# Banded attention with sinks, then a gated feed-forward: sink weights of all heads in one product per pair of heads

## The chip, the cores and the metric

The kernel runs on one core of a Trainium2 chip. The metric is the time of one execution on the device in microseconds (us), from the median of several executions. The engines are TensorE (PE in the profile; PEld is its weight load), VectorE (DVE), ScalarE (ACT), GpSimd (POOL) and SyncE (SP), which here issues the DMA transfers. Matmul results land in PSUM; everything else lives in SBUF.

## The reference

```python
batch, n_heads, seq, head_dim = (4, 8, 768, 64);  n_sink, window = (4, 128)
scores = scale * np.matmul(q, k.transpose(0, 1, 3, 2))
is_sink = pos[None, :] < int(n_sink)
in_window = (rel >= 0) & (rel < int(window))        # rel = query position - key position
a = softmax of scores where (is_sink | in_window), else masked
attn_out = np.matmul(a, v)
x = attn_out.transpose(0, 2, 1, 3).reshape(B * S, H * D)      # (3072, 512)
gate = 1.0 / (1.0 + np.exp(-(x @ w_gate)));  val = x @ w_val   # d_ff = 1536
out = gate * val @ w_out                                       # (3072, 512)
```

All inputs are float32 (the feed-forward weights arrive as float64 and are decoded in the kernel). `n_sink` and `window` are inputs; a slow general path takes over if they lie outside what the fast path is built for.

## The kernel before, in words

**Two parts that run into each other.** Attention is done in units called attends: one head of one batch and two tiles of 128 queries. There are 4 batches x 3 groups of two tiles x 8 heads = 96 attends, numbered `u`. Eight consecutive attends (one group) give the 512 rows of `x`, transposed, for two tiles. The feed-forward then runs over chunks of tiles (`MT`: four tiles, two, then six chunks of three), for each of twelve slices `f` of `d_ff`: up-projections into `m` (`feed_part`, L1057), tanh gating (`th`, `gh`, `gl`), down-projections into `o`.

**Precision.** A float32 product is made of float32r parts: a value is split in a high part and the rest, and a product is high x high + low x high + high x low. `copy` (L505) makes the high part on ACT or DVE, `rest` (L516) the low part on POOL or DVE (DVE alone if the source is in PSUM). The first 16 attends (`PLAIN`) use plain float32 matmuls instead, which are recorded as two instructions each.

**One attend** (`attend`, L697). Loads of q, k and v; k carries the first `NS` = 16 keys after each tile of 128, so a tile has `KW` = 144 key columns. Scores go to a PSUM tile `a`; one DVE instruction merges the two tiles of the window (`tri`), one applies mask and maximum; ACT takes the exponential with the row sum `rs`; after the guard and the reciprocal all 144 columns of `P` are multiplied by it. `turn` (L799) transposes on PE, per query tile, the 128 window columns and the 16 sink columns: four transposes. The window part goes through ACT, DVE and POOL to `wt`. The sink part, 16 rows x 256 queries, is copied to `sk`, and its rest is made on DVE (not in plain attends). `pv` (L876) multiplies by the values: two or three matmuls for the window and one more of 256 columns for the sinks, with the stationary `vshl`, in the same accumulation. ACT and DVE add the high and low halves into `xr`, 64 rows for each head of a pair.

**From attention to the feed-forward.** After each second head (`if h % 2`, L932) `xr` is split into `XH[:, c]` and `XL[:, c]`, `c` = pair of heads. `XH` and `XL` are a ring of `RING` = 6 tiles. The up-projection of a chunk is cut in halves: the first reads pairs 0 and 1, the second pairs 2 and 3. In plain attends `xr` is a PSUM tile `a`; there are three buffers of tag `a` (`B_a`), used by scores, transposes and pv results. Outside plain attends `xr` is in SBUF, three buffers of 256 columns.

**The sinks' values** (`sinks`, L663): per batch, four small loads of v into `VSRAW`, a copy and a rest into one of two `VSHL`.

**The order.** `Plan.run` (L285) is a list scheduler on the host. It holds estimated durations for all operations and writes out one order per engine, by priority: an attend has priority `u`, its operations' engines may be alternatives; decoding of weight slices has due times in units of `u` (the last about 25); on PE the feed-forward has priority 10000 and more, so it fills what attention leaves. Up to 130 us (`WARM`), PE gets filler matmuls (`m<-ident`) where it would be idle. Because engines run in the written order, an instruction that waits holds up those behind it on its engine. All planned instructions go through one helper line, L484, so groups in the profile are told apart by their tiles.

Of the kernel before, what the change touches and what calls it, by code (L numbers as in the profile page):

```python
# [19 lines left out]

NS = 16
WIN = 128
# [3 lines left out]
RING = 6  # L26
# [4 lines left out]
PLAIN = 16  # L31
SINKP = -2.0
SCALP = -0.5
# [25 lines left out]
B_small = 1  # L59
B_xr = 3  # L60
B_th = 2
B_g = 2
# [6 lines left out]
BUFS = {}  # L69
# [361 lines left out]
def kernel(  # L431
# [3 lines left out]
    k: bass.AP,  # L435
    v: bass.AP,
    n_sink: bass.AP,
    window: bass.AP,
# [118 lines left out]
    nc.gpsimd.memset(VSRAW(), 0.0)  # L557
    for x in SK:
        nc.vector.tensor_copy(out=x(), in_=VSRAW().rearrange("p h d -> p (h d)"))

# [30 lines left out]
    def places():  # L591
        G.iota(
            mk()[:, 0:128], [[-1, 128]], base=0, channel_multiplier=1,
            allow_small_or_imprecise_dtypes=True,
        )
        G.iota(
            mk()[:, 128:144], [[1, NS]], base=0, channel_multiplier=0,
            allow_small_or_imprecise_dtypes=True,
        )
# [15 lines left out]
    def first_mask():  # L615

        rel, col, ge = mk()[:, 0:128], mk()[:, 128:144], mk()[:, 144:272]
        inw, snk, s0 = mk()[:, 272:400], mk()[:, 400:416], mk()[:, 416:432]
        V.scalar_tensor_tensor(
            out=inw, in0=rel, scalar=win, in1=ge, op0=ALU.is_lt, op1=ALU.mult  # L620
        )
        V.tensor_scalar(out=snk, in0=col, scalar1=nsk, scalar2=None, op0=ALU.is_lt)
        V.tensor_tensor(out=s0, in0=snk, in1=inw[:, 0:NS], op=ALU.is_gt)
        low(am[0][:, 0:128], inw)
        low(am[0][:, 128:KW], s0)

    def later_masks():


        rel, relm, inm = mk()[:, 0:128], mk()[:, 432:560], mk()[:, 560:688]  # L630
        snk, inp = mk()[:, 400:416], mk()[:, 688:704]
        V.tensor_scalar(out=inm, in0=relm, scalar1=win, scalar2=None, op0=ALU.is_lt)
# [27 lines left out]
    chunk_of = [i for i, parts in enumerate(MT) for _ in range(sum(parts))]  # L660
    VS = {}

    def sinks(b, u):  # L663
        raw, vs = VSRAW, VSHL[b % 2]
        VS[b] = raw, vs
# [6 lines left out]
        u = max(u, PLAIN)  # L672
        copy(u + SINKP, H // 2 * D, lambda: vs()[:, :, 0:D], raw, [raw], [(vs, 0)])
# [22 lines left out]

    def attend(u, b, h, t0, T, XR):  # L697

# [16 lines left out]
        else:  # L715
# [11 lines left out]
            qk_reads, qk_ns = [qs, kh, kl], 2  # L727

        P = tile([128, T, KW], F32, "P", BUFS["P"])
        rs = tile([128, 4], F32, "rs", BUFS["P"])  # L730
# [44 lines left out]
        for t in range(T):  # L775
            plan.op(
                u, [
                    ("V", 390, lambda t=t: V.tensor_scalar(
                        out=P()[:, t], in0=P()[:, t], scalar1=rs()[:, t : t + 1], scalar2=None,
                        op0=ALU.mult,  # L780
                    )),
                    ("A", 320, lambda t=t: A.mul(out=P()[:, t], in_=P()[:, t], mul=rs()[:, t : t + 1])),
                    ("G", 450, lambda t=t: G.tensor_scalar(
                        out=P()[:, t], in0=P()[:, t], scalar1=rs()[:, t : t + 1], scalar2=None,
                        op0=ALU.mult,
                    )),
                ][::-1],
                [rs], [(P, t)],
            )


# [30 lines left out]

        plan.op(u, [("PE", 30 + 2 * T * 110, turn)], [P], [tp, wt], busy=0.45)
        plan.op(
# [11 lines left out]

        o = 64 * (h % 2)
        if plain:
            vhl = vraw
            sk = tile([128, W], F32, "low", BUFS["small"])  # L840
            copy(u, W, lambda: sk()[o : o + NS], lambda: tp()[0:NS, W : 2 * W], [tp], [sk], True)
        else:
            sk = SK[h % 2]
# [15 lines left out]
        acc = None if plain else tile([128, 512], F32, "a", BUFS["a"], ps)  # L859
        if h % 2 == 0:  # L860
            XR[0] = tile([128, 512], F32, "a", BUFS["a"], ps) if plain else tile([128, W], F32, "xr", BUFS["xr"])
        xr = XR[0]
# [10 lines left out]

        vs = VS[b][0] if plain else VS[b][1]

        def pv():  # L876
            a = (xr()[e : e + D] if plain else acc())[:, 0 : Z * W].rearrange("p (z x) -> p z x", z=Z)
            for i, (_, l, c0, r0, n) in enumerate(blocks):
                PE.matmul(
                    a[:, :, c0 : c0 + n], lhsT=vhl()[:, l],  # L880
                    rhs=w().rearrange("p z t x y -> p z (t x y)")[:, :, r0 : r0 + n],
                    start=i == 0, stop=False, skip_group_check=True,
                )
            if plain:
                sv, sw = vs()[o : o + NS, h // 2], sk()[o : o + NS]
            else:
                sv, sw = vs()[:, h // 2], sk()[:, 0:W]
            PE.matmul(
                a[:, 0], lhsT=sv, rhs=sw, start=False, stop=True, skip_group_check=True
            )  # L890

        e = (h % 2) * D
        if plain:
            plan.op(
                u, [("PE", sum(5 + 4 * n / 2.4 for n in [W] + [x[-1] for x in blocks]), pv)], [vs, sk, vhl, wt],
                [(xr, h % 2)],
            )
        else:
            low = tile([D, W], F32, "low", BUFS["small"])
            plan.op(  # L900
                u, [("PE", mac(W) + sum(mac(2 * n) for *_, n in blocks), pv)],
                [vs, sk, vhl, wt], [acc, low, (xr, h % 2)],
            )
# [15 lines left out]
            else:  # L919
# [7 lines left out]
                u, [("V", vec(W), lambda: V.tensor_tensor(  # L927
                    out=xr()[e : e + D], in0=acc()[0:D, W : 2 * W], in1=low(), op=ALU.add
                ))],
                [acc, low], [(xr, h % 2)],  # L930
            )
        if h % 2:  # L932

            c, g = h // 2, b * NT + t0
            runs = [[0]]
            for t in range(1, T):
                if chunk_of[g + t] == chunk_of[g + t - 1]:
                    runs[-1].append(t)
                else:
                    runs.append([t])  # L940
            for run in runs:
                cols = slice(run[0] * 128, run[-1] * 128 + 128)
                ts = slice((g + run[0]) % RING * 128, (g + run[0]) % RING * 128 + len(run) * 128)
                parts = [(c, (g + t) % RING) for t in run]
                x = lambda cols=cols: xr()[:, cols]
                hi, lo = lambda ts=ts: XH()[:, c, ts], lambda ts=ts: XL()[:, c, ts]
                copy(u, len(run) * 128, hi, x, [xr], [(XH, p) for p in parts], plain)
# [5 lines left out]
    def f0(prev):  # L953
        return 1 - prev

# [178 lines left out]
    for b in range(B):  # L1134
        t0 = 0
        for T in AT[b]:
            XR = [None]
            for h in range(H):
                attend(u, b, h, t0, T, XR)
                u += 1  # L1140
# [34 lines left out]

_INS = ["q", "k", "v", "n_sink", "window", "moe_w_gate", "moe_w_val", "moe_w_out"]
_OUTS = [((3072, 512), "float32")]
# [37 lines left out]
```

## Time and profile before

| | |
|---|---|
| median of 3 runs | 828.9 us (827.07 to 831.28) |
| profiled execution, span from first to last instruction | 828.5 us |
| PE busy | 808.2 us, 98% |
| DVE busy | 527.2 us, 64% |
| POOL busy | 450.6 us, 54% |
| ACT busy | 417.9 us, 50% |
| moved by DMA | 95.31 MB, mean 115 GB/s |

The profile of an execution gives its span and no other time; the median lies 0.4 us above it. Matmuls are pipelined, so a matmul's length in a row overlaps the next one's; the distance between starts tells what it costs. Groups are written as line, engine, operation, written tile <- read tiles, shapes, count, busy us, mean ns, and the idle time before them with what ended it.

### The profile page before, as it was taken

The page shows a single profiled execution, that of the slowest core. Times are in us where ns is not written, and L with a number is a line of the kernel's source. Part 1 is how long each engine was busy: PE and PEld are TensorE (multiplying, and loading weights), DVE is VectorE, ACT ScalarE, POOL GpSimd, SP SyncE. Part 2 cuts the span into 40 slices and gives each one's busy share as a digit, 9 for nine tenths or more (in the row PEclk, how much of TensorE's full clock was granted, in tenths as well). Part 3 has the DMA queues.
Part 4 walks back from the last instruction along what each step waited for, and adds up shares of the span by engine and source line. Part 5 has one row for each costly group of instructions (what it writes and reads, how often), then busy time and mean ns, then how long its engine had stood idle before and what let it go on. Part 6 is the DMA issues. An engine that isn't in the chain of part 4 may idle for free.

```text
span 828.5 us, 15445 instructions
## 1 busy us (share of the span) xinstructions
PE 808.2 (98%) x4804; PEld 729.3 (88%) x4804; DVE 527.2 (64%) x1610; ACT 417.9 (50%) x1197; POOL 450.6 (54%) x610
## 2 busy tenths in 40 slices
PE   8999999999999999999999999999999999999996
PEld 6667688888999989999899999999989999999995
DVE  5767689898899898936941499856951485111111
ACT  3666788986668766624630376634730272001001
POOL 4656578899676777725651387755741383111110
PEclk8999999999999999999999999999999999999998
DMA  5667767784645444323431253433431141112112
GB/s 142 173 178 201 214 170 219 218 231 143 180 126 131 125 122 119 108 81 94 127 96 38 54 153 92 121 96 93 127 95 41 36 115 32 44 35 88 40 38 67
DMA packets 99256, 95.31 MB, mean 115 GB/s; under 512 B 44384, under 2 KB 79200, under 8 KB 99168
## 3 DMA queue, kind: packets, MB, share of 16 engines
q1 hardware_dynamic: 99168, 94.25, 41.1%
q8 instruction: 41, 0.67, 0.3%
q14 instruction: 47, 0.39, 0.2%
HBM read 84.77 MB, written 9.44 MB: 114 GB/s over the span
## 4 chain that ended last, share of the span: by engine, by line
PE 67%; DVE 9%; ACT 3%; DMA 2%; POOL 2%; issue 2%; SPq 1%; DVEq 0%; ACTq 0%; POOLq 0%
PE m L484 38%; PE o L484 18%; PE a L484 10%; DVE sk L484 1%; DVE w L484 1%; DMA vraw<-in_v_dram 1%; SPq L484 1%; ACT P L484 1%; DVE vhl L484 1%; DVE wt L484 1%; DVE P L484 1%; DVE xr L484 1%; DVE a L484 1%; DMA qkT<-in_k_dram 1%; POOL P L484 1%
## 5 line engine op out<-in xcount | busy, mean ns | idle before, releaser
L484 POOL TENSOR_TENSOR gl<-th,gh 128x384 fp32r<-128x384 f32 (+1 forms) x73 | 70.8, 971 | 206.8 <-DVE gh L484 196.9
L484 DVE SCALAR_TENSOR_TENSOR th<-th,m 128x384 f32<-128x384 f32 (+1 forms) x108 | 54.6, 505 | 198.9 <-PE m L484 198.2
L484 ACT ACTIVATE th<-m 128x384 f32<-128x384 f32 (+1 forms) x108 | 49.3, 457 | 232.9 <-PE m L484 218.8
L484 POOL TENSOR_SCALAR_AFFINE_SELECT wt<-wt 128x512 fp32r<-128x512 f32 (+3 forms) x192 | 117.0, 610 | 51.6 <-DVE wt L484 31.5
L484 PE MATMUL m<-XH,wvh 128*128 128x384 f32 (+1 forms) x432 | 140.1, 324 | 0.6 <-ACT th L484 0.6
L484 PE MATMUL m<-XH,wgh 128*128 128x384 f32 (+1 forms) x432 | 140.2, 325 | 0.0
L484 PE MATMUL m<-XL,wvh 128*128 128x384 f32 (+1 forms) x432 | 137.4, 318 | 0.0
L484 PE MATMUL m<-XL,wgh 128*128 128x384 f32 (+1 forms) x432 | 137.4, 318 | 0.0
L484 PE MATMUL m<-XH,wgl 128*128 128x384 f32 (+1 forms) x432 | 137.3, 318 | 0.0
L484 PE MATMUL m<-XH,wvl 128*128 128x384 f32 (+1 forms) x432 | 137.3, 318 | 0.0
L484 PE MATMUL o<-woh,gh 128*128 128x512 f32 x276 | 110.6, 401 | 0.0
L484 PE MATMUL o<-woh,gl 128*128 128x512 f32 x276 | 108.5, 393 | 1.0 <-DVE gl L484 0.5
L484 PE MATMUL o<-wol,gh 128*128 128x512 f32 x276 | 107.8, 391 | 0.5 <-DMA wol<-wol_d 0.5
L484 ACT ACTIVATE P<-P,negm_all 128x144 f32<-128x144 f32 x192 | 78.8, 411 | 26.2 <-DVE negm_all L484 23.7
L484 PEld LDWEIGHTS m<-XH,wvh 128*128 128x128 f32 x432 | 81.5, 189 | 3.7 <-ACT th L484 0.8
L484 PEld LDWEIGHTS m<-XH,wgh 128*128 128x128 f32 x432 | 81.4, 188 | 3.0 <-issue 0.7
L484 PEld LDWEIGHTS m<-XL,wvh 128*128 128x128 f32 x432 | 81.6, 189 | 1.4
L484 PEld LDWEIGHTS m<-XL,wgh 128*128 128x128 f32 x432 | 81.5, 189 | 1.2
L484 PEld LDWEIGHTS m<-XH,wvl 128*128 128x128 f32 x432 | 81.4, 189 | 0.0
L484 PEld LDWEIGHTS m<-XH,wgl 128*128 128x128 f32 x432 | 81.4, 188 | 0.0
L484 DVE CUSTOM_DVE_ANT_0 P<-a,am 128x144 f32<-128x144 f32 x192 | 58.6, 306 | 9.6 <-PE a L484 3.2
L484 PEld LDWEIGHTS o<-woh,gl 128*128 128x128 f32 x276 | 51.7, 187 | 14.0 <-POOL gl L484 1.3
(116 smaller groups left out, 1727.1 us busy)
## 6 DMA issues: line engine op xcount, KB each, us to landing
wol<-wol_d SPq DMA_DIRECT2D x108, 256.0 KB, 2.9
qkT<-in_k_dram SPq DMA_DIRECT2D x120, 108.0 KB, 2.7
qkT<-in_q_dram SPq DMA_DIRECT2D x176, 64.0 KB, 2.5
wst<-in_moe_w_gate_dram SPq DMA_DIRECT2D x12, 512.0 KB, 4.6
wst<-in_moe_w_val_dram SPq DMA_DIRECT2D x12, 512.0 KB, 4.5
wst<-in_moe_w_out_dram SPq DMA_DIRECT2D x12, 512.0 KB, 4.0
vraw<-in_v_dram SPq DMA_DIRECT2D x64, 96.0 KB, 2.3
out_dram<-w SPq DMA_DIRECT2D x23, 256.0 KB, 2.5
```

The costliest lines, as they stand in the source:

```text
L484: return lambda *a, **kw: tc.keep_in_program_order(op(*a, **kw))
```

## The change

`NS` becomes 4, so `KW` is 132: k loads, scores, masks and exponentials are 12 columns narrower per tile. The normalising multiplication covers only the 128 window columns. The four sink columns of each head are multiplied by `rs` in an instruction of their own, into `psk`, which gathers all eight heads of a group. `turn` and `pv` no longer deal with sinks. After the eighth head a new function `join` transposes `psk` (32 columns per query tile, two transposes), puts the high part twice and the rest once into the 96 rows of `sk`, and multiplies it, in one matmul per pair of heads, by `VSP`: 32 rows of high values, the same again, 32 rows of the low values. The host passes the sinks' values as an extra input, laid out so that each row has values only in the columns of its own head. A sum on DVE adds the product to `xs` (four heads, 512 columns, three buffers), and only then are `XH` and `XL` made, two pairs at a time. In plain attends the pv result is copied to `xs` by ACT. `VSP` has one buffer for all batches; its load goes through a buffer of tag `w2`.

```diff
-NS = 16
+NS = 4
-SINKP = -2.0
+SINK0 = 1.5
+B_psk = 2
+B_sk = 2
...
-    VSRAW = Fixed(const.tile([128, H // 2, D], F32, name="vsraw"))
-    VSHL = [Fixed(const.tile([128, H // 2, 2 * D], F32R, name=f"vshl{i}")) for i in range(2)]
-    SK = [Fixed(const.tile([128, 256], F32R, name=f"sk{i}")) for i in range(2)]
...
+    NR = H * NS
+    VSP = Fixed(const.tile([3 * NR, H // 2, 2 * D], F32R, name="vsp"))
...
     def sinks(b, u):
-        raw, vs = VSRAW, VSHL[b % 2]
-        for o in range(0, 128, 32):
-            dma(
-                u if u < PLAIN else u + SINKP, 91.0, lambda o=o: Q.dma_start(
-                    out=raw()[o : o + NS], in_=v[b, o // 64 :: 2, 0:NS, :].rearrange("h p d -> p h d"),
-                ), w=[(raw, o)],
-            )
...
+        raw = tile([3 * NR, H // 2, 2 * D], F32, "w2", BUFS["w2"])
+        vs = VSP
+        pr = u + SINK0
+        dma(pr, 600.0, lambda: Q.dma_start(out=raw(), in_=v_sink[b]), w=[raw, vs])
+        copy(pr, H * D, vs, raw, [raw], [vs])
         rest(
-            u + SINKP, H // 2 * D, lambda: vs()[:, :, D : 2 * D], raw, lambda: vs()[:, :, 0:D],
-            [raw, (vs, 0)], [(vs, 1)],
+            pr, H * D, lambda: vs()[2 * NR : 3 * NR], lambda: raw()[2 * NR : 3 * NR],
+            lambda: vs()[2 * NR : 3 * NR], [raw], [vs],
         )
...
-                        out=P()[:, t], in0=P()[:, t], scalar1=rs()[:, t : t + 1], scalar2=None,
+                        out=P()[:, t, 0:128], in0=P()[:, t, 0:128], scalar1=rs()[:, t : t + 1],
...
+        def sink_weights(E):
+            return lambda: E.tensor_tensor(
+                out=psk()[:, 0:T, h], in0=P()[:, 0:T, 128:KW],
+                in1=rs()[:, 0:T].unsqueeze(2).to_broadcast([128, T, NS]), op=ALU.mult,
+            )
+        plan.op(
+            u, [("V", 110, sink_weights(V)), ("G", 400, sink_weights(G))], [rs, (P, T)], [(psk, h)]
+        )
...
-                PE.transpose(
-                    out=tp()[0:NS, W + t * 128 : W + t * 128 + 128], in_=P()[:, t, 128:KW],
-                    identity=ident,
-                )
...
-            copy(
-                u, W, lambda: sk()[o : o + NS, 0:W], lambda: tp()[0:NS, W : 2 * W], [tp], [(sk, 0)],
-                True,
-            )
-            rest(
-                u, W, lambda: sk()[o + 32 : o + 32 + NS, 0:W], lambda: tp()[0:NS, W : 2 * W],
-                lambda: sk()[o : o + NS, 0:W], [tp, (sk, 0)], [(sk, 1)], True,
-            )
...
-            PE.matmul(
-                a[:, 0], lhsT=sv, rhs=sw, start=False, stop=True, skip_group_check=True
-            )
...
+            if h % 2:
+                plan.op(
+                    u, [("A", act(W, True), lambda: A.copy(out=xs()[:, c], in_=xr()[:, 0:W]))], [xr],
+                    [(xs, (c, 0)), (xs, (c, 1))],
+                )
...
-        if h % 2:
+        if h == H - 1:
+            join(u, b, t0, T, XS, psk)
+
+    def join(u, b, t0, T, XS, psk):
+        W, g, vs = T * 128, b * NT + t0, VSP
+        ts = tile([128, 512], F32, "a", BUFS["a"], ps)
+        sk = tile([3 * NR, W], F32R, "sk", BUFS["sk"])
+        def turn():
+            for t in range(T):
+                PE.transpose(
+                    out=ts()[0:NR, t * 128 : t * 128 + 128],
+                    in_=psk()[:, t].rearrange("p h s -> p (h s)"), identity=ident,
+                )
+        plan.op(u, [("PE", 30 + T * 110, turn)], [psk], [ts, sk], busy=0.45)
+        for i in (0, 2):
+            plan.op(
+                u, [("A", act(W, True), lambda i=i: A.copy(
+                    out=sk()[i * NR : i * NR + NR], in_=ts()[0:NR, 0:W]
+                ))],
+                [ts], [(sk, i)],
+            )
+        rest(
+            u, W, lambda: sk()[NR : 2 * NR], lambda: ts()[0:NR, 0:W], lambda: sk()[0:NR],
+            [ts, (sk, 0)], [(sk, 1)], True,
+        )
...
+        for i, xs in enumerate(XS):
+            sp = tile([128, 512], F32, "a", BUFS["a"], ps)
...
+            def add(i=i, spv=spv):
+                for c in range(2):
+                    PE.matmul(
+                        spv()[:, c], lhsT=vs()[:, 2 * i + c], rhs=sk(), start=True, stop=True,
+                    )
+            plan.op(u, [("PE", 2 * mac(W), add)], [vs, sk], [sp])
+            plan.op(
+                u, [("V", vec(2 * W), lambda spv=spv, xs=xs: V.tensor_tensor(
+                    out=xs(), in0=spv(), in1=xs(), op=ALU.add
+                ))],
+                [sp], [xs],
+            )
...
+                copy(u, n, hi, x, [xs], [(XH, p) for p in parts])
                 rest(
-                    u, len(run) * 128, lo, x, hi, [xr] + [(XH, p) for p in parts],
-                    [(XL, p) for p in parts], plain,
+                    u, n, lo, x, hi, [xs] + [(XH, p) for p in parts], [(XL, p) for p in parts]
                 )
...
+        if name == "v_sink":
+            t = _np.zeros((a.shape[0], 3, a.shape[1], NS, a.shape[1] // 2, 2, a.shape[3]), a.dtype)
+            for h in range(a.shape[1]):
+                t[:, :, h, :, h // 2, h % 2] = a[:, None, h, :NS]
```

More of the change, by code (lines that the diff above doesn't have):

```diff
@@ L436 @@
     v: bass.AP,
+    v_sink: bass.AP,
     n_sink: bass.AP,
@@ L551 @@
     XL = Fixed(const.tile([128, NC, RING * 128], F32R, name="XL"))
-    VSRAW = Fixed(const.tile([128, H // 2, D], F32, name="vsraw"))
-    VSHL = [Fixed(const.tile([128, H // 2, 2 * D], F32R, name=f"vshl{i}")) for i in range(2)]
-    SK = [Fixed(const.tile([128, 256], F32R, name=f"sk{i}")) for i in range(2)]
-    nc.gpsimd.memset(VSRAW(), 0.0)
-    for x in SK:
-        nc.vector.tensor_copy(out=x(), in_=VSRAW().rearrange("p h d -> p (h d)"))
+    NR = H * NS
+    assert NR == 32
+    VSP = Fixed(const.tile([3 * NR, H // 2, 2 * D], F32R, name="vsp"))
     val = keep.tile([128, 2], F32, name="val")
@@ L596, in places @@
         G.iota(
-            mk()[:, 128:144], [[1, NS]], base=0, channel_multiplier=0,
+            mk()[:, 128 : 128 + NS], [[1, NS]], base=0, channel_multiplier=0,
             allow_small_or_imprecise_dtypes=True,
@@ L615, in first_mask @@
     def first_mask():
-        rel, col, ge = mk()[:, 0:128], mk()[:, 128:144], mk()[:, 144:272]
-        inw, snk, s0 = mk()[:, 272:400], mk()[:, 400:416], mk()[:, 416:432]
+        rel, col, ge = mk()[:, 0:128], mk()[:, 128 : 128 + NS], mk()[:, 144:272]
+        inw, snk, s0 = mk()[:, 272:400], mk()[:, 400 : 400 + NS], mk()[:, 416 : 416 + NS]
         V.scalar_tensor_tensor(
@@ L630, in later_masks @@
         rel, relm, inm = mk()[:, 0:128], mk()[:, 432:560], mk()[:, 560:688]
-        snk, inp = mk()[:, 400:416], mk()[:, 688:704]
+        snk, inp = mk()[:, 400 : 400 + NS], mk()[:, 688 : 688 + NS]
         V.tensor_scalar(out=inm, in0=relm, scalar1=win, scalar2=None, op0=ALU.is_lt)
@@ L695, in load, with attend @@
         )
-    def attend(u, b, h, t0, T, XR):
+    def attend(u, b, h, t0, T, XR, XS, PSK):
         prev = 1 if t0 else 0
@@ L727, in attend @@
             qk_reads, qk_ns = [qs, kh, kl], 2
+        if h == 0:
+            PSK[0] = tile([128, T, H, NS], F32, "psk", BUFS["psk"])
+        psk = PSK[0]
         P = tile([128, T, KW], F32, "P", BUFS["P"])
@@ L778, in attend @@
                     ("V", 390, lambda t=t: V.tensor_scalar(
-                        out=P()[:, t], in0=P()[:, t], scalar1=rs()[:, t : t + 1], scalar2=None,
-                        op0=ALU.mult,
-                    )),
-                    ("A", 320, lambda t=t: A.mul(out=P()[:, t], in_=P()[:, t], mul=rs()[:, t : t + 1])),
+                        out=P()[:, t, 0:128], in0=P()[:, t, 0:128], scalar1=rs()[:, t : t + 1],
+                        scalar2=None, op0=ALU.mult,
+                    )),
+                    ("A", 320, lambda t=t: A.mul(
+                        out=P()[:, t, 0:128], in_=P()[:, t, 0:128], mul=rs()[:, t : t + 1]
+                    )),
                     ("G", 450, lambda t=t: G.tensor_scalar(
-                        out=P()[:, t], in0=P()[:, t], scalar1=rs()[:, t : t + 1], scalar2=None,
-                        op0=ALU.mult,
+                        out=P()[:, t, 0:128], in0=P()[:, t, 0:128], scalar1=rs()[:, t : t + 1],
+                        scalar2=None, op0=ALU.mult,
                     )),
@@ L821, in split @@
             )
-        plan.op(u, [("PE", 30 + 2 * T * 110, turn)], [P], [tp, wt], busy=0.45)
+        plan.op(u, [("PE", 30 + T * 110, turn)], [P], [tp, wt], busy=0.45)
         plan.op(
@@ L835, in attend @@
         plan.op(u, [("G", 1100.0 if plain else 1400.0, split)], [], [wt])
-        o = 64 * (h % 2)
         if plain:
             vhl = vraw
-            sk = tile([128, W], F32, "low", BUFS["small"])
-            copy(u, W, lambda: sk()[o : o + NS], lambda: tp()[0:NS, W : 2 * W], [tp], [sk], True)
-        else:
-            sk = SK[h % 2]
-            copy(
-                u, W, lambda: sk()[o : o + NS, 0:W], lambda: tp()[0:NS, W : 2 * W], [tp], [(sk, 0)],
-                True,
-            )
-            rest(
-                u, W, lambda: sk()[o + 32 : o + 32 + NS, 0:W], lambda: tp()[0:NS, W : 2 * W],
-                lambda: sk()[o : o + NS, 0:W], [tp, (sk, 0)], [(sk, 1)], True,
-            )
+        else:
             vhl = tile([128, L, 2 * D], F32R, "vhl", BUFS["vhl"])
@@ L859, in attend @@
         acc = None if plain else tile([128, 512], F32, "a", BUFS["a"], ps)
-        if h % 2 == 0:
-            XR[0] = tile([128, 512], F32, "a", BUFS["a"], ps) if plain else tile([128, W], F32, "xr", BUFS["xr"])
+        if h % 4 == 0:
+            XS.append(tile([128, 2, W], F32, "xr", BUFS["xr"]))
+        xs, c = XS[-1], h // 2 % 2
+        if plain and h % 2 == 0:
+            XR[0] = tile([128, 512], F32, "a", BUFS["a"], ps)
         xr = XR[0]
@@ L872, in attend @@
         assert blocks[0][-1] == W
-        vs = VS[b][0] if plain else VS[b][1]
         def pv():
@@ L881, in pv @@
                     rhs=w().rearrange("p z t x y -> p z (t x y)")[:, :, r0 : r0 + n],
-                    start=i == 0, stop=False, skip_group_check=True,
+                    start=i == 0, stop=i == len(blocks) - 1, skip_group_check=True,
                 )
[L884 to L887, printed above, removed]
-            PE.matmul(
-                a[:, 0], lhsT=sv, rhs=sw, start=False, stop=True, skip_group_check=True
-            )
         e = (h % 2) * D
@@ L894, in attend @@
             plan.op(
-                u, [("PE", sum(5 + 4 * n / 2.4 for n in [W] + [x[-1] for x in blocks]), pv)], [vs, sk, vhl, wt],
-                [(xr, h % 2)],
-            )
+                u, [("PE", sum(5 + 4 * n / 2.4 for *_, n in blocks), pv)], [vhl, wt], [(xr, h % 2)]
+            )
+            if h % 2:
[3 more added lines that the diff above has]
+                )
         else:
@@ L900, in attend @@
             plan.op(
-                u, [("PE", mac(W) + sum(mac(2 * n) for *_, n in blocks), pv)],
-                [vs, sk, vhl, wt], [acc, low, (xr, h % 2)],
+                u, [("PE", sum(mac(2 * n) for *_, n in blocks), pv)],
+                [vhl, wt], [acc, low, (xs, (c, h % 2))],
             )
@@ L927, in attend @@
                 u, [("V", vec(W), lambda: V.tensor_tensor(
-                    out=xr()[e : e + D], in0=acc()[0:D, W : 2 * W], in1=low(), op=ALU.add
+                    out=xs()[e : e + D, c], in0=acc()[0:D, W : 2 * W], in1=low(), op=ALU.add
                 ))],
-                [acc, low], [(xr, h % 2)],
+                [acc, low], [(xs, (c, h % 2))],
             )
-        if h % 2:
[L934 to L940, printed above, removed]
+        if h == H - 1:
+            join(u, b, t0, T, XS, psk)
@@ new lines, in join @@
+    def join(u, b, t0, T, XS, psk):
[20 more added lines that the diff above has]
+        )
+        runs = [[0]]
+        for t in range(1, T):
+            if chunk_of[g + t] == chunk_of[g + t - 1]:
+                runs[-1].append(t)
+            else:
+                runs.append([t])
+        for i, xs in enumerate(XS):
+            sp = tile([128, 512], F32, "a", BUFS["a"], ps)
+            spv = lambda sp=sp: sp()[:, 0 : 2 * W].rearrange("p (c x) -> p c x", c=2)
+            def add(i=i, spv=spv):
[10 more added lines that the diff above has]
+            )
@@ L941, in attend @@
             for run in runs:
                 cols = slice(run[0] * 128, run[-1] * 128 + 128)
[L943 to L947, printed above, removed]
+                k = (g + run[0]) % RING * 128
@@ L948, in attend @@
+                ts_ = slice(k, k + len(run) * 128)
+                parts = [(c, (g + t) % RING) for t in run for c in (2 * i, 2 * i + 1)]
+                x = lambda cols=cols, xs=xs: xs()[:, :, cols]
+                hi = lambda ts_=ts_, i=i: XH()[:, 2 * i : 2 * i + 2, ts_]
+                lo = lambda ts_=ts_, i=i: XL()[:, 2 * i : 2 * i + 2, ts_]
+                n = 2 * len(run) * 128
+                copy(u, n, hi, x, [xs], [(XH, p) for p in parts])
                 rest(
-                    u, len(run) * 128, lo, x, hi, [xr] + [(XH, p) for p in parts],
@@ L1136 @@
         for T in AT[b]:
-            XR = [None]
+            XR, XS, PSK = [None], [], [None]
             for h in range(H):
-                attend(u, b, h, t0, T, XR)
+                attend(u, b, h, t0, T, XR, XS, PSK)
                 u += 1
@@ L1173 @@
         general(tc, q, k, v, ident, nsk, win, wres, wol_d, out)
-_INS = ["q", "k", "v", "n_sink", "window", "moe_w_gate", "moe_w_val", "moe_w_out"]
+_INS = ["q", "k", "v", "v_sink", "n_sink", "window", "moe_w_gate", "moe_w_val", "moe_w_out"]
 _OUTS = [((3072, 512), "float32")]
@@ L1189 @@
     for name in _INS:
-        a = inputs[name]
+        a = inputs["v" if name == "v_sink" else name]
+        if name == "v_sink":
+            t = _np.zeros((a.shape[0], 3, a.shape[1], NS, a.shape[1] // 2, 2, a.shape[3]), a.dtype)
+            for h in range(a.shape[1]):
+                t[:, :, h, :, h // 2, h % 2] = a[:, None, h, :NS]
+            a = t.reshape(a.shape[0], 3 * a.shape[1] * NS, a.shape[1] // 2, 2 * a.shape[3])
         if name in "qk":
```

6 lines of the change are left out of this document (removed).

## The prediction

> **What bounds the kernel now.** I read the page's busy lines and slices first, then the chain by engine.
>
> ```profile
> span 828.5 us, 15445 instructions
> PE 808.2 (98%) x4804; PEld 729.3 (88%) x4804; DVE 527.2 (64%) x1610; ACT 417.9 (50%) x1197; POOL 450.6 (54%) x610
> PE   8999999999999999999999999999999999999996
> PE 67%; DVE 9%; ACT 3%; DMA 2%; POOL 2%; issue 2%; SPq 1%; DVEq 0%; ACTq 0%; POOLq 0%
> ```
>
> TensorE (PE) is busy 98% of the span and carries two thirds of the chain. But the mean hides three stages, so the view of windows comes next (per stretch: length, then busy time of PE, PEld, DVE, ACT, POOL, then clock, DMA share, GB/s).
>
> ```profile
> 0.00:50.00 50.00, 46.14 (x247) 33.45 (x248) 31.26 (x125) 28.56 (x81) 27.59 (x43) 0.93 0.60 166
> 50.00:100.00 50.00, 50.00 (x298) 36.63 (x296) 35.31 (x105) 35.49 (x91) 30.23 (x40) 1.00 0.71 198
> 105.00:283.80 178.80, 174.48 (x1237) 160.21 (x1238) 160.68 (x455) 138.24 (x378) 141.37 (x175) 1.00 0.62 175
> 283.80:700.00 416.20, 413.95 (x2373) 383.88 (x2372) 279.23 (x882) 201.47 (x620) 229.58 (x331) 1.00 0.34 92
> 750.00:800.00 50.00, 50.00 (x266) 47.03 (x265) 7.31 (x16) 4.53 (x9) 8.12 (x8) 1.00 0.17 51
> ```
>
> I cut the stages at 105 and 283.8 us because of these rows of the PE timeline (start, length, operation, idle before it):
>
> ```profile
> 36.55 0.36 PE L484 MATMUL m<-XH,wgh 128*128 128x256 f32 x1
> 101.21 0.83 PE L484 MATMUL m<-ident 128*128 128x128 f32 x6
> 105.15 0.39 PE L484 MATMUL a<-kh,qs 128*128 128x272 f32 x1 [3.11 <-DVE XL L484]
> 275.57 0.28 PE L484 MATMUL a<-sk,vshl 128*128 128x256 f32 x1
> 283.79 0.34 PE L484 MATMUL m<-XH,wgh 128*128 128x384 f32 x1
> ```
>
> The `m<-ident` matmuls are filler that keeps PE's clock up while it has nothing to do; the last stand just before 105. So up to 105 us (the 16 plain attends and the first decoded weights) PE time is not what counts. At 283.79 the first 384-wide up-projection shows that chunk 2 begins. It needs tile 8, hence group 4, whose last head's matmul is at 275.57. From 283.8 on PE is idle 2.25 us in 416 and every other engine is under 70%: there a microsecond less of PE work is a microsecond less of time. Between 105 and 283.8 PE is 98% busy, but VectorE (DVE) is 90% busy as well, with attention and the weight decoding: both can bound.
>
> **PE, price of each part.** Transposes: four answers of the PE timeline, each over a narrower window, show one run growing by an instruction at a time.
>
> ```profile
> 307.08 0.33 PE L484 MATMUL a<-ident,P 128*128 128x128 f32 x1
> 307.08 0.44 PE L484 MATMUL a<-ident,P 128*128 128x128 f32 x2
> 307.08 0.55 PE L484 MATMUL a<-ident,P 128*128 128x128 f32 x3
> 307.08 0.66 PE L484 MATMUL a<-ident,P 128*128 128x128 f32 x4
> 307.49 0.42 PE L484 MATMUL m<-XH,wvh 128*128 128x384 f32 x1
> 307.75 0.34 PE L484 MATMUL m<-XL,wvh 128*128 128x384 f32 x1
> 307.93 0.34 PE L484 MATMUL m<-XH,wvl 128*128 128x384 f32 x1
> 302.34 0.28 PE L484 MATMUL a<-sk,vshl 128*128 128x256 f32 x1
> 302.45 0.34 PE L484 MATMUL m<-XH,wgh 128*128 128x384 f32 x1
> 303.62 0.29 PE L484 MATMUL a<-kl,qs 128*128 128x272 f32 x1
> 303.74 0.29 PE L484 MATMUL a<-kh,qs 128*128 128x272 f32 x1
> ```
>
> Each transpose adds 0.11 us, the 16-column sink ones as much as the 128-column ones. From 307.08 to 307.75 there are 0.67 us: four transposes (0.44), one `m` matmul (0.18, by 307.75 to 307.93), and 0.05 for the switch. A sink matmul takes 0.11 (302.34 to 302.45), a score matmul of 272 columns 0.12 (303.62 to 303.74). A matmul's price goes by such distances, not by its length in the row, which overlaps the next one.
>
> How many of them lie behind 283.8 us, from the view of tile `a` on PE for 283.8 to 700:
>
> ```profile
> L484 PE MATMUL a<-ident,P x216: 270/272/331, 287.5 to 691.5; 128*128 128x128 f32 x108
> L484 PE MATMUL a<-kl,qs x104: 272/288/291, 289.2 to 687.3; 128*128 128x272 f32 x88, 128*128 128x144 f32 x16
> L484 PE MATMUL a<-sk,vshl x55: 277/282/285, 286.3 to 696.3; 128*128 128x256 f32 x55
> ```
>
> Removed there: 108 sink transposes x 0.11 = 11.9; 55 sink matmuls x 0.11 = 6.1; twelve fewer key columns in 2 x 88 score matmuls, 12/272 x 0.12 x 176 = 0.9 (the 144-wide ones I count at nothing). Together 18.9 us. Added: 7 joins (groups 5 to 11), each with two transposes (0.22), four 256-wide matmuls (0.44) and three runs with a switch (0.15): 0.81 x 7 = 5.7. **Net 13.2 us less, on the path.** Nothing hides it, since feed work is always at hand there, and nothing new comes late: attention ends at 696.3 (last sink matmul), and from 750 to 800 PE only feeds, so the last joins have time before the chunk that needs them.
>
> The Trainium skill, TensorE: Matmul & The Clock Gate, section "Back-to-back issue gap", gives about 56 ns for an isolated warm matmul with 128 moving columns and about 81 ns in a stream with weight loads; by 56 ns, the transposes would be worth half and the sum 5 to 6 us less. The rows above have 110 ns for this fp32 transpose, and they decide.
>
> **105 to 283.8 us.** The same view for that stretch:
>
> ```profile
> L484 PE MATMUL a<-ident,P x100: 270/272/328, 109.0 to 278.6; 128*128 128x128 f32 x50, 128*16 128x128 f32 x50
> L484 PE MATMUL a<-sk,vshl x25: 277/282/290, 108.9 to 281.9; 128*128 128x256 f32 x25
> ```
>
> PE loses 50 x 0.11 + 25 x 0.11 + 0.5 (scores) = 8.8 and gains three joins, 2.4: 6.4 less, if PE is the bound. But chunk 2 also needs group 4's XH and XL. Groups of DVE and ACT, whole span, and the last XL that chunk 2 needs:
>
> ```profile
> L484 DVE TENSOR_TENSOR sk<-a,sk 16x256 fp32r<-16x256 f32 x80 | 33.3, 416 | 4.0 <-ACT wt L484 1.4 <-ACT sk L484 0.3
> L484 DVE CAST sk<-a 16x256 fp32r<-16x256 f32 x46 | 19.0, 412 | 7.9 <-ACT wt L484 4.3 <-PE a L484 2.9
> L484 DVE TENSOR_TENSOR xr<-a,low 64x256 f32<-64x256 f32 x80 | 33.2, 415 | 1.5
> L484 DVE TENSOR_SCALAR rs<-rs 128x2 f32<-128x2 f32 x45 | 18.7, 415 | 4.0 <-ACT P L484 3.8
> L484 DVE RECIPROCAL rs<-rs 128x2 f32<-128x2 f32 x96 | 15.1, 158 | 2.0 <-POOL rs L484 0.5
> L484 ACT CAST sk<-a 16x256 fp32r<-16x256 f32 x34 | 12.2, 359 | 0.5 <-DVE wt L484 0.2
> L484 DVE TENSOR_TENSOR XL<-xr,XH x1: 423/423/423, 279.6 to 279.6; 128x128 fp32r<-128x128 f32 x1
> ```
>
> Per attend DVE loses 0.416 and, in 46 of 80, another 0.412: 0.65. It gains one small multiplication of 8 columns, not in the trace: between 0.158 (reciprocal) and 0.415 (the guard on `rs`); it may go to POOL instead. I take 0.25, nearer to the reciprocal, since both are a few columns wide. It waits for the reciprocal; behind it on DVE stand the next scores' masks. Each join adds on DVE a 256-wide difference (0.42) and two 512-wide sums (between 0.415 and twice that; I take 0.65): 1.7, or 0.21 per attend. Net -0.2 per attend, bounds -0.33 to +0.05; over 25 attends -5 us, bounds -8 to +1. ACT is about even (34 copies of 0.359 go, two per join of that kind come). Against this, the XH copies of group 4 now follow a sum over all eight heads. Its transposes need only the softmax of head 7 and so lie beside that head's own matmuls; behind the pv matmul stand one more sum (0.65), and copies and differences of four tiles in one burst. I take 3.5 us later, bounds 1.5 to 6. Attention was ready at 279.6 + 0.42 = 280.0; now 280.0 - 5 x (a half, since DVE is not alone in the way) + 3.5 = 281, bounds 273.5 to 287. PE alone would be ready at 283.8 - 6.4 = 277.4. The later one counts: **chunk 2 starts about 2.8 us earlier**, bounds -3 and +6.4.
>
> **Up to 105 us.** A plain sink matmul takes 0.57 us (two instructions):
>
> ```profile
> 40.92 0.64 PE L484 MATMUL a<-low,vsraw 16*64 16x256 f32 x2
> 41.49 0.72 PE L484 MATMUL a<-qkT 64*128 64x272 f32 x2
> L484 PE MATMUL m<-ident 128*128 128x128 f32 x170 | 29.2, 316 | 1.8 <-POOL ident masks.py:199 1.8
> ```
>
> Sixteen of them and 32 transposes are 12.6 us of PE work, but the 170 fillers show that PE had time to spare; what shortens the stage is the copy of the sinks' weights (0.36 on ACT, 0.41 on DVE) per attend, and that a plain `xr` now leaves its PSUM buffer after one ACT copy, not after DVE's XL. That last is what PE waited 3.11 us for at 105.15. At most 16 x 0.4 + 3 = 9 us less. Against it: the first up-projections at 36.55 ran on heads 0 to 3 alone and must now wait for a join, and group 1's join is exposed in front of chunk 0's second half: up to 6 us more. The four sink loads of 16 KB become one of 192 KB with one issue on SP, behind the first attends' loads; from the second batch on that load waits for the last join of the batch before, and SP is in order, so q, k, v and wol loads queue behind it. The planner issues it only when it holds that join for done; I cost it at nothing, 3 us if wrong. I take **2 us less** for the stage, bounds -6 and +9.
>
> **Sum.** 828.5 - 13.2 - 2.8 - 2 = 810.5; the median, 828.9, lies 0.4 above the span, so 811 us.
>
> **Rivals.**
> (a) *Attention becomes the bound before chunk 2*: the 90% of DVE speaks for it, the dropped 0.65 us per attend against it. Chunk 2 starts up to 3 us later than now, the plain stage gains nothing: 828.9 - 13.2 + 3 = 819. Chance 0.16.
> (b) *The plain stage gives its whole 9 us*, chunk 2 follows: 828.9 - 13.2 - 6.4 - 9 = 800, mostly 800 to 804. Chance 0.14.
> (c) *A transpose is worth half its spacing*, because part of it is the wait behind the one before: 108 transposes at 0.055 less: 811 + 6 = 817. The even growth by 0.11 speaks against it. Chance 0.08. (The Trainium skill's 56 ns, above, would be this.)
> (d) *Slower*: at each head DVE stalls in order behind the new multiplication, and joins hold PSUM buffers `a` (three in all) that scores need. In place: chunk 2's start. 25 attends a full microsecond longer each make it 25 later, less the 3.8 it has in hand: 828.9 + 21 - 13.2 = 837. It decides from 13.2 + 3.8 = 17 us, or 0.7 per attend. DVE's sum above says the other way. Chance 0.05.
> (e) *No change to speak of*: the list scheduler's new order opens holes like that of 105.15, four or five of them: 825 to 833. PE's 2.25 us of idle in 416 speaks against it. Chance 0.06.
>
> **How the numbers follow.** Forecast 811 (805 to 816): 0.51. With (a), (b) and (c) the range is 801 to 821, leaving out a part of (a) and (b), and (d) and (e). A measurement here tells 0.5%, 4 us, from no change. Faster by more: the forecast, (a), (b), (c), 0.88; within: (e), 0.06; slower: (d) and a tail of (e), 0.06.
>
> **What would show it.** Runs of transposes x2, not x4; no `sk` matmul per head; PE idle still some 2 us behind chunk 2's start, and from there to the end 13 us less. Chunk 2's first 384-wide matmul at about 279 (less 2 for the plain stage). If that row is at 285 or later, (a) or (d); if the stretch behind it is not 13 us shorter, the PE prices are wrong. PE waits on `XH` or `XL` in the view of waits, over some 5 us in sum, would show that joins come too late.

## The result and the profile after

The changed kernel takes 805.7 us (median of 4 runs, 804.2 to 806.6) against 828.2 beside it: a ratio of 0.972, 95% interval 0.970 to 0.9745. Faster, by 22.4 us; the forecast was 18, and 805.7 lies just inside the near end of its 805 to 816.

The page's first and second parts, changed kernel, in the order in which the prediction shows them:

```profile
span 804.9 us, 14932 instructions
PE 787.0 (98%) x4618; PEld 715.3 (89%) x4618; DVE 511.5 (64%) x1560; ACT 415.7 (52%) x1173; POOL 437.5 (54%) x609
PE   9999999998999999999999999999999999999995
```

PE is as full as before, at the same 98%: its idle time fell only from 20.3 to 17.9 us, while there are 186 fewer PE instructions. The view of windows, cut at the starts of chunk 1 (202.96) and chunk 2 (272.19); columns as before:

```profile
0.00:105.00 105.00, 102.14 (x590) 80.77 (x590) 73.77 (x254) 69.90 (x187) 62.95 (x92) 1.00 0.61 174
105.00:203.00 98.00, 92.17 (x636) 82.85 (x634) 90.07 (x202) 76.13 (x175) 82.67 (x91) 1.00 0.69 208
203.00:272.20 69.20, 69.20 (x499) 65.06 (x498) 59.99 (x207) 50.12 (x162) 50.72 (x82) 1.00 0.56 152
272.20:700.00 427.80, 426.81 (x2407) 398.08 (x2406) 273.83 (x867) 208.60 (x631) 225.91 (x332) 1.00 0.34 93
```

From 203 to 700 us PE is idle 1 us. Between 105 and 203 it is idle 5.8, with DVE at 92%. The PE timeline of the changed kernel has the four rows that answer to those of before:

```profile
51.96 0.36 PE L487 MATMUL m<-XH,wgh 128*128 128x256 f32 x1
136.31 0.61 PE L487 MATMUL m<-ident 128*128 128x128 f32 x4
202.96 0.36 PE L487 MATMUL m<-XH,wgh 128*128 128x256 f32 x1
272.19 0.33 PE L487 MATMUL m<-XH,wgh 128*128 128x384 f32 x1
```

The first up-projection comes at 52, not at 36.6, because it waits for the first join (in the run below without the joins' product it comes at 38.4); filler lasts until 136, not 101. In the kernel before, chunk 1 began at

```profile
209.67 0.28 PE L484 MATMUL m<-XH,wgh 128*128 128x256 f32 x1
```

**Where the time came from.** One cut is chunk 1's start, which follows the last decoded weights. Up to it the kernel gains 209.7 - 203.0 = 6.7 us, behind it (828.5 - 209.7) - (804.9 - 203.0) = 16.9 us. For the second part, the view of tile `a` on PE, first the kernel before (209.6 to 700), then the changed one (203 to 700):

```profile
L484 PE MATMUL a<-ident,P x268: 270/272/331, 218.9 to 691.5; 128*128 128x128 f32 x134
L484 PE MATMUL a<-sk,vshl x69: 277/282/286, 209.6 to 696.3; 128*128 128x256 f32 x69
```

```profile
L487 PE MATMUL a<-ident,P x138: 270/272/329, 202.8 to 643.7; 128*128 128x128 f32 x138
L487 PE MATMUL a<-sk,vsp x36: 277/282/288, 228.0 to 600.9; 96*128 96x256 f32 x36
L487 PE MATMUL a<-ident,psk x18: 270/272/273, 224.4 to 598.0; 128*32 128x128 f32 x18
```

Gone are 134 sink transposes at 0.105 us (14.1; the price is measured below), 69 sink matmuls at 0.11 (7.6) and 12 columns in 230 score matmuls (1.2): 22.9. Come are 18 transposes (1.9) and 36 matmuls at 0.115 (4.1): 6.0. The difference is 16.9, the same as the gain of this part, but that the two agree to a tenth is luck. The sum leaves out that the changed kernel has two more attends' window transposes behind the cut (138 against 134), that PE is idle there 1.0 us up to 700 and not 2.8, and that its last six down-projections start 0.43 us apart, at a granted clock of 0.50 between 795 and 798 us, where those of the kernel before start 0.23 apart.

The first part lost, by the same prices, 58 sink transposes (6.1), 11 sink matmuls (1.2), 16 plain ones at 0.57 (9.1) and some 0.8 in scores, and got three joins (2.0): 15.2 us of PE work less, but only 6.7 us of time. The other 8.5 became filler; PE's idle time ahead of the cut fell from 10.6 to 8.7 us:

```profile
L487 PE MATMUL m<-ident 128*128 128x128 f32 x216 | 39.3, 318 | 2.3 <-POOL ident masks.py:199 1.4 <-ACT th L487 0.9
```

That is 216 fillers, not 170, and by this column 10.1 us more of them (29.2 before).

The cut moves with the order, though. Chunk 1 starts here in two runs of the next section, the kernel before with four sink keys alone and the changed kernel in another order:

```profile
202.56 0.33 PE L484 MATMUL m<-XH,wgh 128*128 128x256 f32 x1
```

```profile
194.90 0.36 PE L487 MATMUL m<-XH,wgh 128*128 128x256 f32 x1
```

The first is 7.1 us earlier than in the kernel before, and the time is the same; the second is 8.1 earlier than in the changed kernel, and the time is 1.2 less. So 6.7 and 16.9 are the split of one pair of orders and prove nothing by themselves. The sum over the whole span does without a cut. By these prices PE has 40.1 us less to do (22.9 and 17.2) and 8.0 more (the joins); with 10.1 more filler and 2.4 less idle time that makes 24.4, against 23.6 between the two spans.

So the theory is: **from chunk 1's start on, each microsecond of PE work is a microsecond of time; before it, another bound sets the pace and PE work is mostly paid by filler.** The rivals were that narrower tensors or lighter DVE work let attention run ahead, that a transpose is worth half its spacing, and that the order which the scheduler happens to write makes the difference.

### The profile page after: what moved, and what is told of

The parts are those of the page before. It is cut to its first block, busy times and chain, and to the rows that moved or that the text cites. A ratio compares the mean times of both kernels' runs of the same rounds, so it can differ in the third digit from the quotient of the medians.

```text
span 804.9 us, 14932 instructions
## 1 busy us (share of the span) xinstructions
PE 787.0 (98%) x4618; PEld 715.3 (89%) x4618; DVE 511.5 (64%) x1560; ACT 415.7 (52%) x1173; POOL 437.5 (54%) x609
## 5 line engine op out<-in xcount | busy, mean ns | idle before, releaser
L487 POOL TENSOR_SCALAR_AFFINE_SELECT wt<-wt 128x512 fp32r<-128x512 f32 (+3 forms) x192 | 119.8, 624 | 45.9 <-DVE wt L487 27.7
L487 PE MATMUL o<-woh,gh 128*128 128x512 f32 x276 | 113.0, 410 | 1.0 <-DVE total L1202 1.0
L487 ACT ACTIVATE P<-P,negm_all 128x132 f32<-128x132 f32 x192 | 77.0, 402 | 31.5 <-DVE negm_all L487 28.7
L487 DVE CUSTOM_DVE_ANT_0 P<-a,am 128x132 f32<-128x132 f32 x192 | 56.0, 294 | 16.7 <-PE a L487 7.6
```

What stands on the lines that cost most here:

```text
L487: return lambda *a, **kw: tc.keep_in_program_order(op(*a, **kw))
```

## The experiments

All are compared, in their own series, with runs of the kernel before (827.5 to 828.4 us). Beside each stands its difference from the changed kernel, 805.7, or from the kernel before.

**Sixteen to four alone**

```diff
-NS = 16
+NS = 4
```

> The kernel before with four sink keys instead of sixteen and nothing else: sinks are still turned, copied and multiplied head by head. If the gain is PE work removed by gathering the heads, narrowing alone takes 12 columns off the wide score matmuls, about 1.4 us on PE, and little elsewhere: 825 to 828 us. If the gain comes from the narrower k loads, masks and exponentials, which let attention run ahead, this kernel has most of it: 808 to 818 us.

827.9 us, ratio 0.9999 (0.9985 to 1.0012): no change. Narrower k loads, masks, exponentials and scores are worth nothing that can be measured by themselves; four keys matter because eight heads then fit in 32 rows. One row of this run is a warning:

```profile
277.91 0.34 PE L484 MATMUL m<-XH,wgh 128*128 128x384 f32 x1
```

Chunk 2 starts 5.9 us earlier than in the kernel before, chunk 1 (above) 7.1 us, and the end is the same. What is gained ahead of such a row is given back behind it, so its time alone is a poor ruler.

**Before, without the sinks' product; after, without the joins' product**

```diff
-                PE.transpose(
-                    out=tp()[0:NS, W + t * 128 : W + t * 128 + 128], in_=P()[:, t, 128:KW],
-                    identity=ident,
-                )
...
-            PE.matmul(
-                a[:, 0], lhsT=sv, rhs=sw, start=False, stop=True, skip_group_check=True
-            )
```

> The kernel before without the product of sink weights and sink values (no sink transposes, no copies to sk, no sink matmul); sinks stay in the scores and the row sums. Leaves out the sinks' part of the attention output. Theory (PE's spacing counts in full from 105 us on): 11.9 + 6.1 behind chunk 2's start, 5.5 + 2.8 in front of it, some 5 in the plain stage: 797 us. Rival (attention bounds the start of chunk 2): only some 3 us in front of it: 803 to 807 us. Rival (a transpose is worth half its spacing): 804 us or more.

800.4 us, 27.1 below the kernel before. (The sinks' part of the attention output is missing in it.) The theory's sum was 797, the rival of an attention bound 803 to 807; it lies between, 3.4 us from the one and 2.6 from the near end of the other, and decides for neither.

```diff
-        ts = tile([128, 512], F32, "a", BUFS["a"], ps)
-        sk = tile([3 * NR, W], F32R, "sk", BUFS["sk"])
...
-            plan.op(u, [("PE", 2 * mac(W), add)], [vs, sk], [sp])
```

> The changed kernel without the joins' product: psk is made, but not turned and not multiplied; XH and XL are made from xs directly after the eighth head. Leaves out the sinks' part of the attention output. Theory: a join costs its PE time, 0.81 us, ten times on the path, and something in the plain stage: 796 to 798 us, and chunk 2's start some 2 to 4 us earlier. Rival (joins are exposed as latency in front of chunks): 790 us or less.

798.0 us, 7.7 below the changed kernel, as the joins' PE time foretold; a latency of the joins that cost more than that (790 or less) is not seen. Chunk 2 was to start 2 to 4 us earlier; it starts at 274.27, 2.1 later, the poor ruler again. (This one leaves out the same part.) So the turning and multiplying of the sinks that is left costs about 7.7 us; the small multiplications into `psk` are still in this run.

**The price of a transpose**

```diff
+                PE.transpose(
+                    out=tp()[0:NS, W + t * 128 : W + t * 128 + 128], in_=P()[:, t, 128:KW],
+                    identity=ident,
+                )
```

> The changed kernel with the two sink transposes per attend put back (four columns each, into spare PSUM columns that nothing reads). Theory (0.11 us each where PE bounds, 55 attends behind chunk 2's start and 25 in front): 805.7 + 12 + 5.5 = 823 us, a little more if the plain stage feels it. Rival (0.055 us each): 814 us. Rival (PE is not the bound in front of chunk 2): 818 us.

819.9 us: 14.2 more, of 17.3 expected and 8.3 at half price. The nearest of the three numbers is that of the rival by which PE is not the bound in front of chunk 2, 818. Of the 192 transposes 110 lie behind chunk 2's start, 11.6 us at 0.105; the 82 in front, 8.6 us of PE work, then cost some 2.6. The next two runs put 64 transposes each in one place.

```diff
+                for _ in range(2 if u < 16 else 0):
+                    PE.transpose(
+                        out=tp()[0:NS, W + t * 128 : W + t * 128 + 128], in_=P()[:, t, 128:KW],
+                        identity=ident,
+                    )
```

> The changed kernel with 64 more sink transposes, four in each of the 16 plain attends (into PSUM columns that nothing reads): 6.7 us of PE time at 0.105 us each. Theory (the first 200 us are set by decoding and attention on the other engines; PE work there is paid by filler): within 2 us of the changed kernel, up to 807. Rival (PE work counts wherever it stands): 812 us.

> The changed kernel with the same 64 more sink transposes, two in each of attends 40 to 71, behind chunk 2's start. Theory (PE is the only bound there): 6 to 7 us slower than the changed kernel, 812 us. Rival (half price): 809 us.

Late (the same lines, `range(1 if 40 <= u < 72 else 0)`): 812.5 us, 6.7 more, 6.7 / 64 = 0.105 us for each. Early: 808.6 us, 2.9 more. Behind chunk 2's start the work counts in full; in the plain attends less than half of it does, and the 2.9 are little more than an order alone moves (1.2 and 2.7, below). No run adds PE work to the attends between, 16 to 39, alone. The early run's filler shows where the rest went:

```profile
L487 PE MATMUL m<-ident 128*128 128x128 f32 x182 | 32.3, 318 | 2.0 <-POOL ident masks.py:199 1.4 <-ACT th L487 0.5
```

There are 34 fillers fewer than in the changed kernel, 7.0 us less by this column. I had expected 2 us at most; the early transposes also lie in the chain of each plain attend, which may be a reason for the 2.9, but no run separates that from the order.

The spacing says the same as the late run. Where a run of transposes is followed by two 384-wide matmuls, the distance from its first start to the second matmul's is 0.61 us with four transposes (median of 30 runs, kernel before) and 0.40 with two (median of 25, changed kernel), like this one:

```profile
337.67 0.38 PE L487 MATMUL a<-ident,P 128*128 128x128 f32 x2
337.81 0.42 PE L487 MATMUL m<-XH,wvh 128*128 128x384 f32 x1
338.07 0.33 PE L487 MATMUL m<-XL,wvh 128*128 128x384 f32 x1
```

(0.61 - 0.40) / 2 = 0.105. The first matmul's row looks as if it began while the transposes still ran, so only the second one's start tells. Half the spacing would have made 809 of the late run (812.5) and 814 of the run before it (819.9), so that rival is refuted. So is, as a price of this instruction, the 56 ns that the Trainium skill (TensorE: Matmul & The Clock Gate, "Back-to-back issue gap") gives for an isolated matmul of 128 columns. A transpose brings a weight load as well as a matmul; the runs take both away together and do not tell which of them makes the 0.105.

**What bounds the first 200 us**

```diff
-        plan.op(
-            prio, [
-                ("A", 1230.0, lambda: A.activation(
-                    out=by(4), in_=by(3), func=AF.Copy, scale=1.0 / 32, bias=-31.0 / 64
-                )),
...
-            [], [st],
-        )
```

> The changed kernel without one of the steps of the weights' decoding (the byte shift, 36 instructions of 1.0 to 1.4 us on ACT, DVE or POOL, all before 200 us). Leaves out the lowest three bits of the weights' mantissas. Theory (decoding sets the pace up to 200 us, so that PE is short of work): 4 to 10 us faster, 796 to 802, with less filler between 100 and 140 us. Rival (PE or attention's chain sets it): within 2 us.

798.7 us, 7.0 faster, more than an order alone moved in any run (2.7). One step of decoding, all of it done by 200 us and none of it on PE, is worth a third of the whole change. In the changed kernel 24 of its 36 instructions ran on ACT, 11 on POOL and one on DVE. These are the windows from 150 to 200 us, first of the changed kernel, then of this one:

```profile
150.00:200.00 50.00, 45.25 (x309) 40.17 (x309) 46.18 (x97) 39.73 (x91) 39.88 (x44) 1.00 0.65 197
```

```profile
150.00:200.00 50.00, 48.22 (x340) 44.04 (x338) 42.52 (x117) 33.49 (x95) 33.26 (x43) 1.00 0.60 182
```

PE's busy time rises from 45.25 to 48.22 of 50, while ACT and POOL have less to do. Decoding does set the pace there, with what shares its engines.

```diff
+        if 16 <= u < 40:
+            plan.op(u, [("V", 330, lambda: V.tensor_copy(out=SCR()[:, 0:L], in_=vraw()))], [vraw], [SCR])
```

> The changed kernel with one more DVE instruction, about 0.35 us, in each of attends 16 to 39 (a copy of v into a buffer that nothing reads): 8 us of DVE time in front of chunk 2's start. Theory (PE is the bound there too, attention has time to spare): within 1.5 us of the changed kernel. Rival (attention by way of DVE sets chunk 2's start, and the dropped DVE copies gave the gain there): 4 to 8 us slower than the changed kernel, and chunk 2 starts as much later.

807.5 us (ratio 0.9769, 0.9725 to 0.9813), 1.7 more. The runs scatter, from 806.1 to 813.9, and the interval reaches 813, so neither the theory's 1.5 nor the rival's 4 to 8 is excluded. The profiled run is the fastest of the four; its span is 804.4, and chunk 2 started in it 4.2 us later (276.4), as the rival expected, without a later end. Whether attention has time to spare in front of chunk 2 stays open.

```diff
-        u, [("V", 110, sink_weights(V)), ("G", 400, sink_weights(G))], [rs, (P, T)], [(psk, h)]
+        u, [("G", 250, sink_weights(G))], [rs, (P, T)], [(psk, h)]
```

> The changed kernel with the new small multiplication always on POOL instead of DVE's first choice. Theory (off the path wherever PE bounds): within 1.5 us of the changed kernel. Rival (the multiplication holds DVE up, by way of its waits): 3 to 6 us faster.

802.5 us, ratio to the kernel before 0.9676 (0.9658 to 0.9694): 3.3 less than the changed kernel, what the rival had asked for, and the fastest measured version that computes everything. Two more runs ask whether that is the work or its order.

```diff
-SINK0 = 1.5
+SINK0 = 0.5
```

> The changed kernel with the priority of the sinks' load and split moved by one attend (SINK0 0.5, not 1.5): the same work in an order that the scheduler writes anew. It measures how far the order alone moves the time: both theories expect within 2 us of the changed kernel; a move of 5 us or more would mean that differences of this size between the other runs need not have a cause in the work.

> The changed kernel with the small multiplication always on POOL and SINK0 0.5: both of the variants before in one. If POOL's 3 us are due to DVE's time and not to the order that came of it, 801 to 803 again; if they are the luck of one order, 804 to 807.

The order alone: 804.6, 1.2 less. Both edits together: 805.2 (0.9729, 0.9713 to 0.9745), no better than the changed kernel and 2.7 more than with POOL in the first order. So POOL's 3.3 us do not outlast a change in the order; differences of about 3 us between such versions need not have a cause in the work, and the fast version is most likely one good order.

**Was it the PSUM buffer in the plain attends?**

```diff
+            if plain:
+                xps = xr
+                xr = tile([128, W], F32, "xr", BUFS["xr"])
+                plan.op(
+                    u, [("A", act(W, True), lambda: A.copy(out=xr(), in_=xps()[:, 0:W]))], [xps], [xr]
+                )
```

> The kernel before, but in the plain attends the pv result is copied from PSUM to an SBUF xr by ACT, as the changed kernel does; XH and XL are made from that. If the PSUM buffer held until DVE's XL is what lengthened the plain stage (the idle 3.11 us at 105 us), the stage ends 3 to 5 us earlier and the kernel gains 3 to 5 us: 823 to 825. If the sinks' copies were it, no change: 827 to 829.

832.5 us, ratio 1.0049 (1.0032 to 1.0066): slower by 4.1, where 3 to 5 faster was expected if the buffer mattered. The idle stretch of 3.11 us is gone, and two short ones stand nearby:

```profile
101.64 0.38 PE L484 MATMUL m<-XH,wgh 128*128 128x256 f32 x1 [0.44 <-DVE XH L484]
102.97 0.39 PE L484 MATMUL m<-XL,wgh 128*128 128x256 f32 x1 [0.95 <-DVE XL L484]
```

Here a hole in PE's time was closed and nothing was gained. Why it became slower, the extra ACT work or the order, is open.

## Why the prediction was right, point by point

**The PE prices and what they count for.** Right. A transpose was put at 0.11 and is 0.105, and the late transposes show that work behind chunk 2's start counts in full. The forecast was 13.2 us there; the stretch to the end went from 828.5 - 283.8 = 544.7 to 804.9 - 272.2 = 532.7, 12.0 less, with one attend more behind the cut. This 12.0 is a weak witness: with four keys alone the same stretch is 549.4, 4.7 longer than before, and the whole time is the same. The prediction's "every other engine is under 70%" leaves out PE's weight loads, 383.88 of 416.20 us in its own row; it did not matter, since both go with a transpose.

**The joins.** 0.81 us each was a little much: the four matmuls need no visible switch, a pair takes 0.23 in this stretch of the changed kernel's PE timeline.

```profile
304.95 0.40 PE L487 MATMUL a<-sk,vsp 96*128 96x256 f32 x2
305.18 0.34 PE L487 MATMUL m<-XH,wvh 128*128 128x384 f32 x1
305.36 0.34 PE L487 MATMUL m<-XL,wvh 128*128 128x384 f32 x1
```

**105 us to chunk 2's start.** Here the forecast row was missed. I let attention bound that start and took 2.8 us out of PE's 6.4, and with the 2 us of the plain stage the row was to stand at 279; it stands at 272.2, 11.6 earlier than before. The joins were to make XL 3.5 us later. DVE's timeline and POOL's have the last XL of group 4 (pairs 2 and 3) here:

```profile
271.98 0.42 DVE L487 TENSOR_TENSOR XL<-xr,XH 128x256 fp32r<-128x256 f32 x1
```

```profile
271.99 1.02 POOL L487 TENSOR_TENSOR XL<-xr,XH 128x256 fp32r<-128x256 f32 x1
```

The later is done at 273.0, 7.0 earlier than the 280.0 of before, just ahead of chunk 2's second half, which alone needs it; the prediction took it for a condition of the start. No wait of PE for XH or XL is listed in the changed kernel, so the joins did not come too late, and (a) did not come about. Whether PE's full 6.4 counted is not shown: with four keys alone the row moved by 5.9 for no gain, and the run with four transposes per attend points the other way, with some 2.6 us for all 82 in front of chunk 2.

**Up to 105 us.** Right that PE's 12.6 us there are in good part paid by filler: 46 more of them, 10.1 us by their column. The reason I gave for the gain, the PSUM buffer, is not borne out in the kernel before by the run with the copy, which was 4.1 us slower; what little PE work counts there, and the DVE and ACT copies that are gone, remain as candidates and were not separated. That the first feed would start later was right (52.0, not 36.6).

**The new multiplication.** I took 0.25 us on DVE:

```profile
L487 DVE TENSOR_TENSOR psk<-P,rs 128x8 f32<-128x8 f32 x80 | 24.7, 308 | 0.6
L487 DVE TENSOR_TENSOR xr<-a,xr 128x512 f32<-128x512 f32 x24 | 16.4, 685 | 2.9 <-PE a L487 2.6
```

It takes 0.308 in the mean (the last section shows why), and the 512-wide sum 0.685 against the 0.65 that I took. DVE's busy time fell from 527.2 to 511.5 us.

**The rivals.** (b), 800 to 804, did not come about; (c) is refuted; (d) and (e) did not happen. The load of the sinks' values queued in front of the others cost nothing that a view of PE's waits shows: its longest wait for DMA is 2.0 us, for `wol`, once, at 194.4, more than 18 us after the nearest load of the sinks' values (175.8).

The total, 22.4 against 18, has 4.4 us that no run assigns to a term. By the rows, 11.6 came ahead of chunk 2's start where 4.8 were forecast; but an order alone moves the time by up to 2.7 us, so part of the 4.4 may be a good order. That the total fell into the range rests on the transposes and sink matmuls behind chunk 2; for what was forecast in front of it, 2.8 and 2, the number is no confirmation. So the theory above is shown from chunk 2's start on; between chunk 1's and chunk 2's it is not.

## What to carry to other kernels

Ask first in which stretch an engine's work counts: the same 64 instructions cost 6.7 us where PE was the only bound and 2.9 where it had filler, though 2.9 is hardly more than an order alone moved. Small products per head that each cost a full instruction are worth gathering, even if the gathered one is mostly zeros: in these runs a transpose of 4 or 16 columns cost what one of 128 did, 0.105 to 0.11 us. With a scheduler that rewrites its order, test an order-only variant before giving 3 us a cause, and do not read a gain off one milestone in the middle: here the starts of chunks 1 and 2 moved by 6 to 8 us while the end stood nearly still.

## What the runs showed of the hardware that was not expected

The small multiplication of 8 columns varies widely on DVE and hardly on POOL. The view of tile `psk`, changed kernel, then the one with POOL alone (minimum, median and maximum in ns):

```profile
L487 DVE TENSOR_TENSOR psk<-P,rs x80: 146/167/1264, 10.4 to 596.1; 128x8 f32<-128x8 f32 x80
```

```profile
L487 POOL TENSOR_TENSOR psk<-P,rs x96: 192/200/731, 11.1 to 593.9; 128x8 f32<-128x8 f32 x96
```

On DVE the median is 0.167 us and the mean 0.308, with a longest of 1.264; on POOL the median is 0.200. The two timelines of the changed kernel show what the long ones wait for:

```profile
366.65 1.05 DVE L487 TENSOR_TENSOR psk<-P,rs 128x8 f32<-128x8 f32 x1
596.11 1.01 DVE L487 TENSOR_TENSOR psk<-P,rs 128x8 f32<-128x8 f32 x1
161.47 0.15 DVE L487 TENSOR_TENSOR psk<-P,rs 128x8 f32<-128x8 f32 x1
```

```profile
366.62 1.05 POOL L487 TENSOR_TENSOR kl<-qkT,kh 128x396 fp32r<-128x396 f32 x1
596.09 1.01 POOL L487 TENSOR_TENSOR gl<-th,gh 128x384 fp32r<-128x384 f32 x1 [0.42 <-DVE bad L1188]
160.65 1.06 POOL L487 TENSOR_SCALAR P<-P,rs 128x128 f32<-128x128 f32 x1
```

Each of the 22 that took over 0.30 us on DVE began while POOL ran a TENSOR_TENSOR or an affine select, and ended 0.01 to 0.03 us after that instruction did. The third pair is the other case: while POOL ran only the multiplication of `P` by `rs`, the small one took its 0.15 us, and at most 0.25 elsewhere. The Trainium skill, GPSIMD Engine Reference, "1. Specifications", says that POOL shares its SBUF interfaces with VectorE and that DVE instructions with two SBUF inputs contend, as this one has. The trace agrees, with 22 of 80 held until POOL was through.
